# Seven half products for a second expert's first layer, and shared row buffers for attention

## Chip, cores and metric

The kernel runs on one core of a Trainium2 chip. Times are device microseconds (us) of that core, the median of several runs. The engines are TensorE (PE, with its weight loads as PEld), VectorE (DVE), ScalarE (ACT), GpSimd (POOL) and SyncE (SP), which issues most of the transfers to memory; they run beside each other and wait for each other by semaphores.

## What is computed

Attention with eight heads, three over all earlier keys and five over a window of 64 keys and four sinks, and behind it a layer of four experts, each of two matrix products with a relu between them, weighted by given probabilities.

```python
# attention: q, k, v are (4, 8, 768, 64)
scores = scale * np.matmul(q, k.transpose(0, 1, 3, 2))
scores = np.where(mask[None, :, :, :], scores, -1000000000.0)
a = softmax(scores)                       # (cut: written out in the reference)
attn_out = np.matmul(a, v)
# experts: x is (3072, 512), w1 (4, 512, 1024), w2 (4, 1024, 512)
p = domain_probs / (domain_probs.sum(-1, keepdims=True) + 1e-09)
for e in range(E):
    h = np.maximum(x @ w1[e], 0.0)
    out += p[:, e:e + 1] * (h @ w2[e])
```

## The kernel before

There are 24 tiles of 128 tokens. Attention works on eight groups of three tiles. The first four tiles go through the experts plainly; the other twenty go as ten *pairs* of tiles. The steps of attention for later groups are put between the steps of the pairs, by a plan of estimated times, so that TensorE always has work.

A pair has two layers. In layer 1 the inputs, scaled by the expert's probability, are multiplied with w1. For experts 0 to 2 this is done plainly, as four steps of eight products of 128 x 128 weights with 256 columns. For expert 3 (`EW`) it is done in Winograd's form of Strassen's scheme: the matrices are cut into 2 x 2 blocks, and seven products of half size stand in for eight. Each of the seven is eight TensorE instructions of 128 columns. The scheme needs sums of blocks of the weights (made once), of the inputs and of the results (made for every pair, on VectorE and ScalarE). Layer 2 uses the same scheme for all experts at once.

```python
EW = E - 1
t1sb = pers.tile([P, 3, KH, FN], FP16, name="t1sb")       # sums of expert 3's weights
...
def plain_layer1(e):
    xs = scaled(e)
    for f0 in range(0, FTP, 2):
        ps = bank()
        for f in range(2):
            for ct in range(DMP):
                nc.tensor.matmul(out=ps[:, f * PC : (f + 1) * PC], ...)   # 256 columns
        nc.scalar.activation(out=blocks[...], in_=ps..., func=AF.Relu)
        step_done()
        yield 2 * DMP * mm_ns(PC), 0.5
...
def winograd_layer1():
    ...
    x = pO.tile([P, DM], FP32, name="pO", bufs=2)
    y = pO.tile([P, DM], FP32, name="pO", bufs=2)
    # keep: a ScalarE copy of a bank; add: a VectorE add of bank and copy, and a maximum with 0
    product(x, w1_part(0, 0), x_part(0, 0), True)
    keep(0, x)
    yield ns, 0.5
    product(y, w1_part(1, 0), x_part(0, 1), True)
    add(0, y, 0)
    yield ns, 0.5
    product(x, t(1), x_sum(1), False)
    keep(1, x)
    yield ns, 0.5
    product(y, t(0), x_sum(0), True)
    keep(2, y)
    minus(x_part(0, 1), x_part(0, 1), x_sum(1))
    yield ns, 0.5
    product(x, w1_part(0, 1), x_part(1, 0), False)
    add(2, x, 3)
    yield ns, 0.5
    product(y, w1_part(1, 1), x_part(0, 1), False)
    add(1, y, 2)
    yield ns, 0.5
    product(x, t(2), x_part(1, 1), False)
    nc.scalar.activation(out=block(1), in_=x..., func=AF.Relu)
    yield ns, 0.5

scale_inputs(nt0, 1)
...
products = winograd_layer1()
n = 0
for e in range(E - 1):
    if e == 1:
        scale_inputs(nt0, 2)
    elif e == 2 and nxt is not None:
        load_probs(nxt)
    for step in plain_layer1(e):
        yield step
        step = next(products, None) if n > 1 else None   # one half product behind a plain step
        n += 1
        if step is not None:
            yield step
    if e:
        sums += input_sums(...)       # S1 = A21 + A22 and S3 = A11 - A21, in two pieces each
...
# layer 2: seven products of 16 instructions of 256 columns; beside them S2, S4,
# and the scaling of the next pair's inputs for experts 0 and 3
```

`product(..., False)` adds onto what is in the bank, so it must come after the reader of the bank's earlier content. Two lines record many operations: `minus` (L939) is every difference, and `scale_inputs` (L1066) every scaling.

Attention's rows of q and k come by transfers of GpSimd's queue into buffers of their own, and SyncE's transposing transfers turn them into `qT`, of which there are two, and `kT`:

```python
def load_q(b, c):
    q16[b, c] = att.tile([P, 3, H, D], FP16, name="q16", bufs=1)
    load_by_rows(q, q16[b, c], b, c)
def load_k(b, c):
    k_rows[b, c] = att.tile([P, 3, H, D], FP16, name="k_rows", bufs=1)
    load_by_rows(k, k_rows[b, c], b, c)
def alloc_qT(b, c):
    qTs[b, c] = att.tile([P, HP, CH], FP16, name="qT", bufs=2)
...
# in attention(), after the fourth of eight heads (group 2 and later):
if n == 3 and more and g > 1:
    transpose_rows(*more)             # kT, then qT, of the next group
```

Of the kernel before, what the change touches and what calls it, by code (L numbers as in the profile page):

```python
# [1 line left out]

# [15 lines left out]
def kernel(  # L18
# [33 lines left out]
    nc = tc.nc  # L52
# [58 lines left out]
    EW = E - 1  # L111
    KH, FN = DMP // 2, F // 2
    t1sb = pers.tile([P, 3, KH, FN], FP16, name="t1sb")
# [18 lines left out]
    XS = 3 * DMP * 2 * P  # L132
    early = moe.tile([P, XS], FP16, name="early", tag="xs", bufs=1)
# [19 lines left out]
    v_sinks = pers.tile([NS, 1, NSH * P], FP16, name="v_sinks")  # L153
# [62 lines left out]
    def load_q(b, c):  # L216
        q16[b, c] = att.tile([P, 3, H, D], FP16, name="q16", bufs=1)
        load_by_rows(q, q16[b, c], b, c)
# [12 lines left out]
    def load_k(b, c):  # L231
        k_rows[b, c] = att.tile([P, 3, H, D], FP16, name="k_rows", bufs=1)
        load_by_rows(k, k_rows[b, c], b, c)
# [3 lines left out]
    def alloc_qT(b, c):  # L237
        qTs[b, c] = att.tile([P, HP, CH], FP16, name="qT", bufs=2)
# [12 lines left out]
    def transpose_rows(b, c):  # L251
        alloc_qT(b, c)
        for x, xr, at in ((kT, k_rows[b, c], P), (qTs[b, c], q16[b, c], 0)):
            for j in range(3):
                nc.sync.dma_start(
                    out=x[:, :, at + j * P : at + (j + 1) * P],
                    in_=xr[:, j, :, :].rearrange("p h d -> p (h d)"),
                    transpose=True,
                )
# [226 lines left out]
    qt16 = att.tile([P, H, 3, D], FP16, name="q16", bufs=1)  # L486
# [38 lines left out]
    def attention(b, c):  # L525
# [109 lines left out]
        def scores(h):  # L635
            hp = h // 2
            es_of[h] = []
            for cols, parts, masks in score_tiles(h):
                ps = bank()
                if first and not es_of[h]:  # L640
                    warm_up(ps, {0: 5, 2: 8}.get(h, 0), P)
                ns = 0
                for n, (t, o, q0, nq) in enumerate(parts):
                    nc.tensor.matmul(  # L644
                        out=ps[:, o : o + nq],
                        lhsT=key_tile(b, c, h, t),
                        rhs=qTs[b, c][:, hp, q0 : q0 + nq],
                        start=(n == 0 or not first),
                        stop=not first,
                        skip_group_check=first,  # L650
                    )
                    ns += mm_ns(nq)
                if first:
                    for m, mo, o0, o1 in masks:
                        bias = bC if m is mC else bSf
                        nc.tensor.matmul(
                            out=ps[:, o0:o1], lhsT=ident16,
                            rhs=bias[:, mo : mo + o1 - o0],
                            start=False, stop=True, skip_group_check=True,
                        )  # L660
                es = att.tile([P, 512], FP16, name="es", bufs=8)
                nc.scalar.activation(  # L662
                    out=es[:, 0:cols], in_=ps[:, 0:cols], func=AF.Exp, scale=SC
                )
                for m, mo, o0, o1 in () if first else masks:
                    nc.vector.tensor_tensor(  # L666
                        out=es[:, o0:o1],
                        in0=es[:, o0:o1],
                        in1=m[:, mo : mo + o1 - o0],
                        op=ALU.mult,  # L670
                    )
                es_of[h].append((es, parts))
                if first:
                    tick(LAG)
                yield ns
# [158 lines left out]
        else:  # L834
# [16 lines left out]
            for n, h in enumerate(order):  # L851
# [12 lines left out]
                if n == 3 and more and g > 1:  # L864
                    transpose_rows(*more)
                if not by_dma and n in (1, 3):
                    yield from transposes({1: 3, 3: 2}[n])
            if more:
                if g == 1:
                    load_probs(pair0)  # L870
                    transpose_rows(*more)
# [75 lines left out]
    def w1_part(j, k):  # L947
        return w1sb[:, EW * DMP + j * KH : EW * DMP + (j + 1) * KH, k * FN : (k + 1) * FN]

    def first_weight_sums():  # L950

        t = [t1sb[:, n, :, :] for n in range(3)]
        return [
            lambda: minus(t[0], w1_part(0, 1), w1_part(0, 0)),
            lambda: minus(t[1], w1_part(1, 1), t[0]),
            lambda: minus(t[2], w1_part(1, 0), t[1]),
            lambda: minus(w1_part(0, 1), w1_part(1, 1), w1_part(0, 1)),
        ]
# [91 lines left out]
    def scaled(e):  # L1050
        n = 2 if e == EW else e % 2
        x = xs_of[0][:, n * DMP * PC : (n + 1) * DMP * PC]
        return x.rearrange("p (c x) -> p c x", c=DMP)

    def scale_inputs(nt0, e):

        if xs_of[0] is None:
            xs_of[0] = moe.tile([P, XS], FP16, name="xs", tag="xs", bufs=1)
# [11 lines left out]
    def x_part(i, j):  # L1070
        return scaled(EW)[:, j * KH : (j + 1) * KH, i * P : (i + 1) * P]
# [6 lines left out]
    def scaled_sums():  # L1078
        nc.vector.tensor_tensor(
            out=x_sum(0), in0=x_part(1, 0), in1=x_part(1, 1), op=ALU.add  # L1080
        )
        minus(x_sum(1), x_sum(0), x_part(0, 0))
        minus(x_part(1, 0), x_part(0, 0), x_part(1, 0))

    def input_sums(k0, k1):
        k = slice(k0, k1)

        def s1():
            nc.vector.tensor_tensor(
                out=S1[:, k, :], in0=A21[:, k, :], in1=A22[:, k, :], op=ALU.add  # L1090
            )

        return [
            s1,
            lambda: minus(S3[:, k, :], A11[:, k, :], A21[:, k, :]),
        ]
# [4 lines left out]
    def pair_steps(nt0, nxt):  # L1101

        sums = []

        def step_done():
            if sums:
                sums.pop(0)()

        def plain_layer1(e):
            xs = scaled(e)  # L1110
            for f0 in range(0, FTP, 2):
# [19 lines left out]
                step_done()  # L1131
                yield 2 * DMP * mm_ns(PC), 0.5

        def winograd_layer1():

            s = moe.tile([P, 4 * HN], FP32, name="s1", tag="sums", bufs=1)
            kept = [s[:, (n % 2) * HT * P : (n % 2 + 1) * HT * P] for n in range(3)]
            x = pO.tile([P, DM], FP32, name="pO", bufs=2)
            y = pO.tile([P, DM], FP32, name="pO", bufs=2)
# [17 lines left out]
            def block(n):  # L1157
                return blocks[:, n, EW * HT : (EW + 1) * HT, :]
# [12 lines left out]
            def t(n):  # L1171
                return t1sb[:, n, :, :]

            product(x, w1_part(0, 0), x_part(0, 0), True)
            keep(0, x)
            yield ns, 0.5
            product(y, w1_part(1, 0), x_part(0, 1), True)
            add(0, y, 0)
# [6 lines left out]
            minus(x_part(0, 1), x_part(0, 1), x_sum(1))  # L1185
            yield ns, 0.5
            product(x, w1_part(0, 1), x_part(1, 0), False)
            add(2, x, 3)
            yield ns, 0.5
            product(y, w1_part(1, 1), x_part(0, 1), False)  # L1190
            add(1, y, 2)
            yield ns, 0.5
            product(x, t(2), x_part(1, 1), False)
# [5 lines left out]
        scale_inputs(nt0, 1)  # L1199
        if nt0 == pair0:  # L1200
            sums.append(lambda: last_weight_sum(E - 1))
        products = winograd_layer1()
        n = 0
        for e in range(E - 1):
            if e == 1:
                scale_inputs(nt0, 2)
            elif e == 2 and nxt is not None:
                load_probs(nxt)
            for step in plain_layer1(e):
                yield step  # L1210
                step = next(products, None) if n > 1 else None
                n += 1
                if step is not None:
                    yield step
            if e:
                sums += input_sums(0, 2 * HT) if e == 1 else input_sums(2 * HT, 4 * HT)
        for op in sums:
            op()
# [3 lines left out]
        s = s.rearrange("p (n x) -> p n x", n=4)  # L1222
        x = pO.tile([P, DM], FP32, name="pO", bufs=2)[:, 0:HN]
        y = pO.tile([P, DM], FP32, name="pO", bufs=2)[:, 0:HN]
# [36 lines left out]

        def fourth_sum(n):
            k = slice(n * KT // 2, (n + 1) * KT // 2)
            minus(S4[:, k, :], A12[:, k, :], S2[:, k, :])
# [9 lines left out]
        add(0, y, 0, 0)  # L1274
        yield half
        yield from product(x, S2, t(1), False)
        keep(1, x)
        fourth_sum(0)
        yield half
        yield from product(y, S1, t(0), True)  # L1280
        keep(2, y)
        fourth_sum(1)
# [8 lines left out]
        if nxt is not None:  # L1291
            scale_inputs(nxt, EW)
# [6 lines left out]
        if nxt is not None:  # L1299
            scaled_sums()  # L1300
# [8 lines left out]
    def moe_steps():  # L1309
        for e in range(E):  # L1310
            if e == 1:
                turn_probs()
            yield from plain_steps(0, 3, e, lambda: xT[0], (e % 2) * FTP * CH)
            weight_sums(e)
        sums = first_weight_sums()
        for e in range(E):
            n0 = (e % 2) * FTP * P
            for n, step in enumerate(plain_steps(3, 1, e, lambda: xT[1][:, :, 0:P], n0)):
                yield step
                if n == FTP - 1:  # L1320
                    sums[e]()
            if e + 1 < E:
# [3 lines left out]
                    lambda: scale_inputs(pairs[0], EW),  # L1326
                    scaled_sums,
# [14 lines left out]
    def loads(a):  # L1342
        b, c = divmod(a, NCH)
        load_k(b, c)
        load_q(b, c)
# [6 lines left out]
    PAIR = (E - 1) * FTP * DMP * mm_ns(PC) + 28 * FTP // 4 * mm_ns(P) + 7 * KT * mm_ns(HN)  # L1352
# [91 lines left out]
```

The softmax here doesn't subtract the row's maximum and nothing guards it: scores larger than these inputs give would overflow.

## Time and profile before

| | before |
|---|---|
| time, median of 3 | 382.71 us (381.86 to 383.02) |
| span of the profiled execution | 380.0 us |
| busy: POOL | 110.8 us |
| TensorE's clock | 1.0 throughout |
| first pair begins | 91.4 us |
| VectorE idle ahead of its adds of half products (L1161), waiting for TensorE | 16.3 us |

The span is what the profiler recorded of one execution, and is a little shorter than the time. A busy share tells how much of the span an engine worked, not whether others waited for it; the chain that ended last tells that. A group of instructions is one line of the program, one engine and one form of tile: its total, its count, its mean, and how long the engine stood idle just ahead of it. The times of single stages are read from the chain and from stretches of the trace.

### The profile page before, as it was taken

How to read it: one execution, taken by the hardware profiler on the slowest of the kernel's cores; microseconds unless marked ns; L12 is line 12 of the kernel's file. 1: busy time of each engine (PE TensorE's matmuls, PEld its weight loads, DVE VectorE, ACT ScalarE, POOL GpSimd, SP SyncE). 2: the span in 40 equal slices, each digit the busy share in tenths (PEclk: the TensorE clock that was granted, in tenths of full speed). 3: DMA queues.
4: the chain of work that ended last, by engine and by line, in shares of the span. 5: the costliest groups of instructions: out<-in, count | busy, mean ns of one | idle time of the engine just before them, and what ended most of it. 6: DMA issues, size and time to landing. Idle time of an engine off the chain costs nothing.

```text
span 380.0 us, 9930 instructions
## 1 busy us (share of the span) xinstructions
PE 370.4 (97%) x4054; PEld 311.5 (82%) x4054; DVE 267.9 (70%) x590; ACT 230.3 (61%) x476; POOL 110.8 (29%) x152
## 2 busy tenths in 40 slices
PE   7989999999999999999999999999999999999996
PEld 4755556577998998899988998999988998998995
DVE  7745687598978678967667767967767757665560
ACT  4853567656776876665764775675665684541630
POOL 8932662854139029113800118203100000000000
PEclk9999999999999999999999999999999999999999
DMA  9999999999499969965950869965510210110001
GB/s 165 155 208 201 183 192 190 149 191 136 67 136 127 133 99 100 145 124 38 155 81 16 109 123 84 142 127 43 84 54 16 68 58 0 58 57 29 28 2 55
DMA packets 127193, 39.20 MB, mean 103 GB/s; under 512 B 116232, under 2 KB 120876, under 8 KB 127148
## 3 DMA queue, kind: packets, MB, share of 16 engines
q0 software_dynamic: 86816, 19.01, 56.8%
q1 hardware_dynamic: 38732, 19.18, 22.9%
q8 instruction: 31, 0.51, 0.6%
q10 hardware_dynamic: 1600, 0.39, 0.5%
q14 instruction: 14, 0.11, 0.1%
HBM read 44.88 MB, written 6.34 MB: 135 GB/s over the span
## 4 chain that ended last, share of the span: by engine, by line
PE 85%; DMA 7%; POOL 3%; DVE 3%; ACT 1%; issue 0%; POOLq 0%
PE pO L1228 32%; PE pA L1115 27%; PE pO L1145 8%; DMA w2sb<-in_moe_w_dram 7%; PE pO L1004 6%; PE pA L644 5%; PE pA L983 4%; PE pV L756 2%; PE pV L692 2%; POOL vS L302 1%; DVE xs L1066 1%; POOL vR L296 1%; ACT es L662 1%; DVE kS L282 0%; POOL early L441 0%
## 5 line engine op out<-in xcount | busy, mean ns | idle before, releaser
L1115 PE MATMUL pA<-xs,w1sb 128*128 128x256 f16 x960 | 119.1, 273 | 0.2 <-DVE xs L1066 0.2
L1228 PEld LDWEIGHTS <-hA 128*128 128x128 f16 x1120 | 106.5, 98 | 12.8
L1115 PEld LDWEIGHTS <-w1sb 128*128 128x128 f16 x960 | 89.7, 98 | 9.8 <-DVE xs L1066 0.4
L1124 ACT ACTIVATE hA<-pA 128x512 f16<-128x512 f32 x120 | 71.4, 597 | 37.9 <-PE pA L1115 36.2
L662 ACT ACTIVATE es<-pA 128x384 f16<-128x384 f32 (+2 forms) x122 | 59.0, 511 | 32.1 <-PE pA L644 28.0
L1228 PE MATMUL pO<-w2sb,hA 128*128 128x256 f16 x640 | 78.1, 273 | 0.0
L298 POOL DMA_DIRECT2D vS<-in_v_dram x30 | 29.6, 989 | 124.7 <-PE pV L756 117.3
L1228 PE MATMUL pO<-tsb,hA 128*128 128x256 f16 x480 | 58.9, 272 | 0.0
L1066 DVE TENSOR_TENSOR xs<-xT,pB 128x1024 f16<-128x1024 f16 (+1 forms) x52 | 49.4, 969 | 0.0
L939 DVE TENSOR_TENSOR hA<-hA 128x1024 f16<-128x1024 f16 x60 | 39.7, 685 | 0.8
L996 ACT ACTIVATE hA<-pA 128x384 f16<-128x384 f32 (+1 forms) x64 | 22.3, 386 | 20.3 <-PE pA L983 19.5
L1161 DVE TENSOR_TENSOR hA<-pO,s 128x512 f16<-128x512 f32 x30 | 20.6, 687 | 17.2 <-PE pO L1145 16.3
L983 PE MATMUL pA<-xT,w1sb 128*128 128x384 f16 (+1 forms) x256 | 31.7, 273 | 0.1
L1004 PE MATMUL pO<-w2sb,hA 128*128 128x512 f16 x128 | 30.5, 379 | 0.6 <-DMA w2sb<-in_moe_w_dram 0.6
L779 DVE TENSOR_TENSOR xT<-pV,rc 64x384 f16<-64x384 f32 x37 | 20.5, 554 | 14.1 <-ACT rc L784 11.8
L774 ACT ACTIVATE rc<-pV,eps 64x384 f32<-64x384 f32 x37 | 21.3, 575 | 9.1 <-PE pV L756 8.5
L983 PEld LDWEIGHTS <-w1sb 128*128 128x128 f16 x256 | 19.3, 98 | 8.4 <-issue 0.5
L1145 PE MATMUL pO<-xs,w1sb 128*128 128x128 f16 x320 | 24.4, 219 | 0.0
L644 PE MATMUL pA<-qT,kR 128*128 128x384 f16 (+2 forms) x120 | 22.9, 278 | 0.9 <-ACT qT L555 0.4
L1249 DVE TENSOR_TENSOR o<-pO,s 128x256 f32<-128x256 f32 x30 | 12.7, 422 | 14.6 <-PE pO L1228 11.8
L666 DVE TENSOR_TENSOR es<-es,mS 128x384 f16<-128x384 f16 (+1 forms) x40 | 13.4, 343 | 13.4 <-ACT es L662 13.3
L1004 PEld LDWEIGHTS <-hA 128*128 128x128 f16 x128 | 11.9, 98 | 12.6 <-issue 0.8
(131 smaller groups left out, 460.3 us busy)
## 6 DMA issues: line engine op xcount, KB each, us to landing
pB<-p_rows SPq DMA_DIRECT2D x10, 512.0 KB, 3.4
out_dram<-o SPq DMA_DIRECT2D x19, 256.0 KB, 4.6
w1sb<-in_moe_w_dram POOLq DMA_DIRECT2D x8, 512.0 KB, 10.3
w2sb<-in_moe_w_dram POOLq DMA_DIRECT2D x4, 1024.0 KB, 13.3
vS<-in_v_dram POOLq DMA_DIRECT2D x30, 112.0 KB, 3.7
k_rows<-in_k_dram POOLq DMA_DIRECT2D x18, 128.0 KB, 4.6
q<-in_q_dram POOLq DMA_DIRECT2D x18, 128.0 KB, 5.6
vR<-in_v_dram POOLq DMA_DIRECT2D x24, 48.0 KB, 5.3
```

The lines of the kernel that those rows point to most:

```text
L298: gp.dma_start(out=t[:, :, own_v(h)], in_=windows_of(v, b, h, c))
L644: nc.tensor.matmul(out=ps[:, o : o + nq], lhsT=key_tile(b, c, h, t), rhs=qTs[b, c][:, hp, q0 : q0 + nq], start=(n == 0 or not first), stop ...
L662: nc.scalar.activation(out=es[:, 0:cols], in_=ps[:, 0:cols], func=AF.Exp, scale=SC)
L939: nc.vector.tensor_tensor(out=out, in0=a, in1=b, op=ALU.subtract)
L983: nc.tensor.matmul(out=pss[ft][:, 0:cols_n], lhsT=w1sb[:, e * DMP + ct, ft * P : (ft + 1) * P], rhs=x[:, ct, :], start=(n == 0), stop=(n = ...
L996: nc.scalar.activation(out=hs[:, ft, :], in_=ps[:, 0:cols_n], func=AF.Relu)
L1004: nc.tensor.matmul(out=ps_o, lhsT=hs[:, ft, j * P : (j + 1) * P], rhs=w2sb[:, e * FTP + ft, :], start=(ft == 0), stop=(ft == FTP - 1),)
L1066: nc.vector.tensor_tensor(out=o, in0=xin, in1=pb.to_broadcast([P, DMP, n, P]), op=ALU.mult)
L1115: nc.tensor.matmul(out=ps[:, f * PC : (f + 1) * PC], lhsT=w1sb[:, e * DMP + ct, (f0 + f) * P : (f0 + f + 1) * P], rhs=xs[:, ct, :], start= ...
L1124: nc.scalar.activation(out=blocks[:, b0 : b0 + 2, k0 : k0 + 2, :].rearrange("p t f x -> p f t x"), in_=ps.rearrange("p (f t x) -> p f t x" ...
L1145: nc.tensor.matmul(out=ps[:, f * P : (f + 1) * P], lhsT=w[:, ct, f * P : (f + 1) * P], rhs=a[:, ct, :], start=(first and f == 0 and ct == ...
L1228: nc.tensor.matmul(out=ps, lhsT=a[:, k, :], rhs=b(k), start=(first and k == 0), stop=(k == KT - 1), skip_group_check=not first,)
```

## The change

Expert 2's first layer is to be done in the seven half products too, so that two experts are plain and two are not. Expert 2's weight sums are made once, beside the plain tiles. The 14 half products of a pair stand two by two (sometimes one) ahead of each of the eight plain steps, first those of expert 3, then those of expert 2, which uses the two banks exchanged; the second product of each expert goes into one of the four banks of `bank()`. S1 is made in four pieces, one for each expert, and S3 moves to layer 2 as S3 = A22 - S2. All four experts' scaled inputs now have space of their own.

To make room for the added sums and inputs, attention's rows of q and k share one buffer (`rows`), `qT` has one buffer in place of two, `es` (the exponentials) has seven in place of eight, and the sinks of v lie in a part of another tile. So k is transposed after the fourth head as before, q is loaded behind that, and is transposed after the last head's scores.

```diff
-    EW = E - 1
+    EW = (E - 1, E - 2)
-    t1sb = pers.tile([P, 3, KH, FN], FP16, name="t1sb")
+    t1sb = pers.tile([P, len(EW), 3, KH, FN], FP16, name="t1sb")
...
     def load_q(b, c):
-        q16[b, c] = att.tile([P, 3, H, D], FP16, name="q16", bufs=1)
+        if b * NCH + c == NCH:
+            q16[b, c] = moe.tile([P, 3, H, D], FP16, name="q16", tag="o", bufs=1)
+        else:
+            q16[b, c] = att.tile([P, 3, H, D], FP16, name="rows", bufs=1)
...
-        k_rows[b, c] = att.tile([P, 3, H, D], FP16, name="k_rows", bufs=1)
+        k_rows[b, c] = att.tile([P, 3, H, D], FP16, name="rows", bufs=1)
...
-        qTs[b, c] = att.tile([P, HP, CH], FP16, name="qT", bufs=2)
+        qTs[b, c] = att.tile([P, HP, CH], FP16, name="qT", bufs=1)
...
-                es = att.tile([P, 512], FP16, name="es", bufs=8)
+                es = att.tile([P, 512], FP16, name="es", bufs=7)
...
                 if n == 3 and more and g > 1:
-                    transpose_rows(*more)
+                    transpose_k(*more)
+
+                    load_q(*more)
...
             if more:
                 if g == 1:
                     load_probs(pair0)
-                    transpose_rows(*more)
+                    transpose_k(*more)
+                transpose_q(*more)
             for h in waiting:
                 yield from values(h)
...
-            product(y, w1_part(1, 0), x_part(0, 1), True)
-            add(0, y, 0)
+            z = bank()
+            product(z, w1_part(e, 1, 0), x_part(e, 0, 1), True)
+            add(0, z, 0)
...
+        a, b = (winograd_layer1(e, *y) for e, y in zip(EW, (banks, banks[::-1])))
+        n01 = itertools.chain(plain_layer1(0), plain_layer1(1))
+        for steps, op in (
+            ((a, a, n01), lambda: scale_inputs(nt0, EW[1])),
+            ((a, a, n01), lambda: scale_inputs(nt0, 1)),
+            ((a, n01), lambda: scaled_sums(EW[1])),
+            ((a, a, n01), lambda: load_probs(nxt) if nxt is not None else None),
+            ((b, b, n01), lambda: first_sum(0)),
+            ((b, b, n01), lambda: first_sum(EW[0])),
+            ((b, n01), lambda: last_weight_sum(E - 1) if nt0 == pair0 else None),
+            ((b, b, n01), None),
+        ):
+            for x in steps:
+                yield next(x)
+            if op is not None:
+                op()
+        first_sum(1)
+        first_sum(EW[1])
...
+        y = pO.tile([P, DM], FP32, name="pO", bufs=2)[:, 0:HN]
         x = pO.tile([P, DM], FP32, name="pO", bufs=2)[:, 0:HN]
-        y = pO.tile([P, DM], FP32, name="pO", bufs=2)[:, 0:HN]
...
+        def third_sum(n):
+            k = slice(n * KT // 2, (n + 1) * KT // 2)
+            minus(S3[:, k, :], A22[:, k, :], S2[:, k, :])
...
-        fourth_sum(0)
+        third_sum(1)
...
-    PAIR = (E - 1) * FTP * DMP * mm_ns(PC) + 28 * FTP // 4 * mm_ns(P) + 7 * KT * mm_ns(HN)
+    PAIR = 2 * FTP * DMP * mm_ns(PC) + 2 * 7 * HT * KH * mm_ns(P) + 7 * KT * mm_ns(HN)
```

`PAIR` is the plan's estimate of a pair's length; the plan's other numbers stay.

## The prediction, as it stood before the result

> **What bounds the kernel now.** I read the page's shares first, then the groups with shapes kept apart, then the chain that ended last, then busy time by stage, then the order of instructions in one pair. The shares and the chain's summary:
>
> ```profile
> PE 370.4 (97%) x4054; PEld 311.5 (82%) x4054; DVE 267.9 (70%) x590; ACT 230.3 (61%) x476; POOL 110.8 (29%) x152
> ...
> PE 85%; DMA 7%; POOL 3%; DVE 3%; ACT 1%; issue 0%; POOLq 0%
> ```
>
> TensorE (PE) is busy 97% of the span and carries 85% of the chain, so only less TensorE work, or a wait put into TensorE's order, moves the time. VectorE (DVE) is second with 70%. The groups that carry the first layer of the pairs and the vector work beside it:
>
> ```profile
> L1115 PE MATMUL pA<-xs,w1sb 128*128 128x256 f16 x960 | 119.1, 273 | 0.2 <-DVE xs L1066 0.2
> ...
> L1145 PE MATMUL pO<-xs,w1sb 128*128 128x128 f16 x320 | 24.4, 219 | 0.0
> ...
> L1161 DVE TENSOR_TENSOR hA<-pO,s 128x512 f16<-128x512 f32 x30 | 20.6, 687 | 17.2 <-PE pO L1145 16.3 <-ACT s L1155 0.6
> ...
> L1167 DVE TENSOR_SCALAR hA<-hA 128x512 f16<-128x512 f16 x30 | 9.8, 328 | 1.0
> ```
>
> The means (273, 219 ns) contain the pipeline and are no cost. The cost comes from the chain in the last pair, where no attention lies between:
>
> ```profile
> 350.93 2.62 PE pA L1115 x24
> ...
> 364.54 12.24 PE pO L1228 x112
> ```
>
> 24 plain products of 256 columns take 2.62 us: 0.873 us for a step of eight, 109.2 ns each. Layer 1 lasts 364.54 - 350.93 = 13.61 us and holds 12 plain steps and 7 half products, so a half product (eight products of 128 columns) takes (13.61 - 12 x 0.873) / 7 = 0.447 us, 55.9 ns each. All of it is TensorE without a gap. Busy time by stage (columns: stretch, its length, then PE, PEld, DVE, ACT) for layer 1 of the first and the last pair:
>
> ```profile
> 91.44:106.42 14.98, 14.98 (x202) 13.85 (x200) 13.62 (x35) 11.68 (x22) 1.03 (x1) 1.00 0.57 80
> ...
> 350.93:364.54 13.61, 13.61 (x154) 12.52 (x153) 7.38 (x14) 8.86 (x16) 0.00 (x0) 1.00 0.08 28
> ```
>
> VectorE is busy 7.4 us of 13.6 in a pair alone, but already 13.6 of 15.0 in the first pair, where a group of attention runs beside it. TensorE waits for it in neither.
>
> [...] The trace agrees (55.9 and 109.2), so a product of half the width costs 51%, and 7 half-size products cost less than the 8 they replace. [...] In the stretches of the trace that I read, vector instructions ran in program order, one at a time. [...] the trace has 0.685 for 1024 and 0.285 for 256, whose straight line gives 0.42 too.
>
> **The change part by part.** *TensorE, per pair:* removed are 4 plain steps, 4 x 0.873 = 3.49 us; added are 7 half products, 7 x 0.447 = 3.13 us. Saved: 0.36 us a pair, 3.6 us for ten pairs. Nothing else of TensorE changes, so 379.1 us if nothing new waits. That is 0.95% and the ceiling of the gain.
>
> *ScalarE, per pair:* minus 4 x 0.597, plus 3 copies x 0.583 and one relu of 0.593: even.
>
> *VectorE, per pair:* plus 3 adds x 0.687, 3 maxima x 0.328, one difference x 0.283, three scaled sums (0.286 + 0.292 + 0.283): 4.2 us; cutting the first sum into four pieces of 0.42 in place of two of 0.685 adds 0.3. The third sum moves from layer 1 to layer 2. So 4.5 us x 10, and 4 x 0.68 for the weight sums of expert 2: 267.9 + 48 = about 316 us. On average it fits (82% of the span); but pairs 0 to 7 held 176 us of VectorE in 233.7 us (by stage), and would hold 212 in 231: 92%.
>
> *The new order in a pair alone.* Between the end of the second half product and the first product of expert 2, which overwrites the bank of the sixth, TensorE has 4 plain steps and 5 half products: 4 x 0.873 + 5 x 0.447 = 5.73 us. In that time VectorE must run, in this order and by start-to-start times of the last pair: 0.27 from TensorE's end to the add, add and maximum 0.94, scaling for expert 2 1.14, difference 0.21, scaling for expert 1 1.14, add and maximum 0.94, three scaled sums 0.74, and the add that frees the bank 0.69. Sum 6.07. TensorE waits 6.07 - 5.73, with the release some 0.36 us. In the second half expert 2's products have only 3.7 us of VectorE work beside 6.6 of TensorE and don't wait. So in a pair alone the wait eats the gain.
>
> *With attention.* Layer 1 of pairs 0 to 7 held 86.6 us of VectorE, 27.5 more than eight times 7.38; TensorE's stretches are 118.8 long, 9.9 more than eight times 13.61. If half of each falls in the first half of the layer, VectorE's chain there grows by 13.8 and TensorE by 5.0: up to 8.8 us of further waiting. I take half, 4.4, since part of that work can run ahead while the chain still waits for TensorE.
>
> *Buffers.* q can be loaded only after k's transposes have read the shared rows, and transposed only after the last scores, as qT has one buffer. In group 3 the k transposes are issued to 102.7:
>
> ```profile
> 98.07 4.64 SPq L255 DMA_TRANSPOSE kT<-k_rows  x3
> 102.80 3.84 SPq L255 DMA_TRANSPOSE qT<-q  x3
> ```
>
> Landing takes 4.0 from issue, so the last lands at about 105.5; three q loads to 108.1, landing (5.6 from issue) at about 112.9; three transposes, the last issued at 115.3, landed at 119.3. Group 3's first scores ran at 116.08: up to 3 us of waiting. For group 4 the same sum gives 148.5 against 148.03; groups 5 and 7 have 20 us of slack, group 6 some 2. I take 1.5 in all, as these issues may land faster (2.4 is the least seen) and TensorE will itself be later.
>
> Sum of everything: 382.7 - 3.6 + 3.6 + 4.4 + 1.5 = 388.6.
>
> **Rivals.** *A: all hidden.* VectorE starts its work early enough and only TensorE's saving shows: 379.1. For it: the shares (VectorE far from full), and the change's own care (a spare bank for the second product, banks exchanged for the second expert, the third sum moved to layer 2). Against it: 6.07 over 5.73, which holds in every pair. *B: VectorE becomes the bound beside attention*, in full: 8.8 and 3.0 in place of 4.4 and 1.5, 394.5. For it: 13.62 of 14.98 us busy in the first pair before anything is added. Against it: layer 2 has loose waits and can take the overhang. *C: ScalarE's copies come late.* A copy now has one half product and one plain step, 1.32 us, before its bank is accumulated onto, where it had 2.19; an exponential of 0.5 and a relu of 0.6 ahead of it would make it late by 0.3, at perhaps five places: 1 or 2 us. *D: the transposes of q come last everywhere* (the next group held for each): plus 3 to 6 us.
>
> **Range and chances.** I weigh A (379.1) at 0.4 against my sum (388.6) at 0.6: 384.8, rounded to 384.6. A range of 8 in 10: 379.5 to 391. Faster by over 2% (below 375.1) would need more than the TensorE saving: 0.02. Slower by over 2% (above 390.4) needs B or D nearly whole: 0.19. Within 2%: 0.79.
>
> **What would show it.** Plain products fall from 960 to 640 and half products rise from 560 to 1120; PE instructions 4054 to 4294; VectorE about 714 instructions, 312 to 318 us. Layer 1 of the last pair stays near 13.6 us, with a TensorE gap of 0.3 to 0.4 ahead of expert 2's first half product, ended by a vector add; if there is no gap and it lasts 13.25, A is right. In the first pair the gap is above 1 us. TensorE's first scores of group 3 would be held by qT. I am wrong if TensorE's idle time in the pairs stays near nothing, or if the waits lie at ScalarE's copies.

## The result and the profile after

The changed kernel takes 398.72 us (median of 6 runs, 398.02 to 400.37) against 382.74 for the kernel before (median of 6): a ratio of 1.0424, 95% interval 1.0401 to 1.0447. It is slower by 4.2%, and outside the predicted range of 379.5 to 391.

The page of the changed kernel: busy shares, the chain's shares, and the groups of layer 1. Lines have moved: half products are L1144 (L1145 before), their adds L1160, the scaling of inputs L1078, all differences L951.

```profile
PE 372.4 (94%) x4294; PEld 312.3 (79%) x4294; DVE 306.9 (77%) x714; ACT 229.6 (58%) x476; POOL 110.4 (28%) x152
...
PE 56%; DVE 26%; DMA 9%; issue 3%; ACT 3%; POOL 1%; SPq 1%; DVEq 0%; ACTq 0%; POOLq 0%
...
L1115 PE MATMUL pA<-xs,w1sb 128*128 128x256 f16 x640 | 82.9, 273 | 0.0
...
L1144 PE MATMUL pO<-xs,w1sb 128*128 128x128 f16 x480 | 36.6, 219 | 2.4 <-DVE hA L1160 1.8
...
L1160 DVE TENSOR_TENSOR hA<-pO,s 128x512 f16<-128x512 f32 x40 | 27.4, 686 | 6.6 <-PE pO L1144 6.0
```

Counts are as worked out: 640 plain products, 4294 TensorE and 714 VectorE instructions. VectorE's time, 306.9 us, is below the 312 to 318 that were forecast: the forecast added durations, as if VectorE's instructions ran one at a time, and neighbours overlap a little (below, a scaling of 1.22 us begins at 98.86 and the next instruction at 100.00, 0.08 before its end). VectorE is busy only 77%, and yet it carries 26% of the chain where it had 3%. The longest of TensorE's waits (us in total, times, longest), and the group of the seventh half products, from the groups with shapes kept apart:

```profile
PE pO L1144 <- DVE hA L1160: 9.7, 15, 1.5
```

```profile
L1144 PE MATMUL pO<-xs,t1sb 128*128 128x128 f16 x160 | 12.2, 219 | 8.2 <-DVE hA L1160 7.9
```

Of 9.7 us that TensorE waits for adds, 7.9 stand ahead of the product that uses the scaled inputs and the summed weights, the seventh: it accumulates onto the bank that the second add, that of the fifth product, must have read. Busy time by stage, layer 1 of the first and of the last pair:

```profile
92.75:110.04 17.29, 14.93 (x224) 13.74 (x220) 15.62 (x44) 11.60 (x22) 3.67 (x4) 1.00 0.89 112
...
366.96:380.69 13.73, 13.55 (x178) 12.54 (x176) 10.54 (x24) 8.85 (x16) 0.00 (x0) 1.00 0.09 33
```

The first pair's layer 1 grew from 14.98 to 17.29 us, the last pair's from 13.61 to 13.73. What happens in the first pair is seen in the order of time (start, duration, engine, line, tile; in brackets the idle time just before and who ended it):

```profile
98.73 0.62 PE L1144 MATMUL pO<-xs,w1sb 128*128 128x128 f16 x8 [0.50 <-DVE xs L951]
...
98.86 1.22 DVE L1078 TENSOR_TENSOR xs<-xT,pB 128x1024 f16<-128x1024 f16 x1
100.00 0.68 DVE L1160 TENSOR_TENSOR hA<-pO,s 128x512 f16<-128x512 f32 x1
...
100.73 0.61 PE L1144 MATMUL pO<-xs,t1sb 128*128 128x128 f16 x8 [1.20 <-DVE hA L1160]
...
102.32 0.68 DVE L1160 TENSOR_TENSOR hA<-pO,s 128x512 f16<-128x512 f32 x1
...
103.06 0.61 PE L1144 MATMUL pO<-xs,w1sb 128*128 128x128 f16 x8 [0.66 <-DVE hA L1160]
```

The product at 98.73 is the sixth; it waited for a difference of inputs. The seventh waits until the add that began at 100.00 is through, and that add stood behind a scaling of 1.22 us for expert 1. The first product of expert 2, at 103.06, waits for the next add, the third.

VectorE is late from the start of the layer. In the first pair it has attention's work ahead of the first add, the copies of keys above all; in the last pair it only waits for ScalarE's copy:

```profile
93.39 0.61 DVE L291 COPY kS<-kT 64x1736 f16<-64x1736 f16 x1
...
96.20 0.68 DVE L1160 TENSOR_TENSOR hA<-pA,s 128x512 f16<-128x512 f32 x1
...
368.27 0.69 DVE L1160 TENSOR_TENSOR hA<-pA,s 128x512 f16<-128x512 f32 x1 [0.50 <-ACT s L1154]
```

So the first add begins 3.45 us into the layer, against 1.31 in the last pair. From there to the third add VectorE has no idle time of even 0.08 us, in any of the ten pairs: in this half of the layer it is the bound engine.

The whole loss by place, from the first product of each layer to that of the next (attention's steps between them are counted in; all in us):

| | start of the first pair | ten layers 1 | ten layers 2 and the end | span |
|---|---|---|---|---|
| before | 91.28 | 143.95 | 144.77 | 380.0 |
| after | 92.75 | 157.39 | 146.16 | 396.3 |
| difference | +1.5 | +13.4 | +1.4 | +16.3 |

TensorE's saving, 3.6, lies in layer 1, so the waits there are 17.1. The idle time that the trace records in these layers is less, 12.9, since it counts from the modelled end of a product (219 ns after its start, where the next could start after 56). Attention's share of the layers hardly moved: 235 of its TensorE instructions lie in them, against 232 before.

### The profile page after: what moved, and what is told of

It reads as the page before. It is cut to its first block, busy times and chain, and to the rows that moved or that the text cites. A ratio compares the mean times of both kernels' runs of the same rounds, so it can differ in the third digit from the quotient of the medians.

```text
span 396.3 us, 10589 instructions
## 1 busy us (share of the span) xinstructions
PE 372.4 (94%) x4294; PEld 312.3 (79%) x4294; DVE 306.9 (77%) x714; ACT 229.6 (58%) x476; POOL 110.4 (28%) x152
## 4 chain that ended last, share of the span: by engine, by line
PE 56%; DVE 26%; DMA 9%; issue 3%; ACT 3%; POOL 1%; SPq 1%; DVEq 0%; ACTq 0%; POOLq 0%
PE pO L1228 24%; PE pA L1115 10%; PE pO L1144 8%; DVE xs L1078 7%; DMA w2sb<-in_moe_w_dram 7%; DVE hA L1160 4%; PE pA L653 4%; PE pO L1017 3%; PE pA L996 3%; DMA qT<-rows 2%; DVE kS L291 2%; DVE es L675 1%; PE pV L765 1%; PE pV L701 1%; ACT es L671 1%
## 5 line engine op out<-in xcount | busy, mean ns | idle before, releaser
L1228 PEld LDWEIGHTS <-hA 128*128 128x128 f16 x1120 | 106.2, 98 | 12.6
L1115 PE MATMUL pA<-xs,w1sb 128*128 128x256 f16 x640 | 82.9, 273 | 0.0
L1124 ACT ACTIVATE hA<-pA 128x512 f16<-128x512 f32 x80 | 47.8, 599 | 29.5 <-PE pA L1115 27.3
L1115 PEld LDWEIGHTS <-w1sb 128*128 128x128 f16 x640 | 58.9, 98 | 5.5
L1078 DVE TENSOR_TENSOR xs<-xT,pB 128x1024 f16<-128x1024 f16 (+1 forms) x52 | 49.5, 970 | 0.0
L1144 PEld LDWEIGHTS <-w1sb 128*128 128x128 f16 x640 | 39.6, 98 | 5.9 <-issue 3.4
L1144 PEld LDWEIGHTS <-t1sb 128*128 128x128 f16 x480 | 29.3, 98 | 13.1 <-issue 10.2
L951 DVE TENSOR_TENSOR hA<-hA 128x1024 f16<-128x1024 f16 x60 | 39.0, 684 | 0.2
L1144 PE MATMUL pO<-xs,w1sb 128*128 128x128 f16 x480 | 36.6, 219 | 2.4 <-DVE hA L1160 1.8
L212 POOL DMA_DIRECT2D rows<-in_q_dram x15 | 13.4, 900 | 86.8 <-DMA kT<-rows 86.8
L1154 ACT COPY s<-pO 128x512 f32<-128x512 f32 x60 | 33.6, 591 | 6.1 <-PE pO L1144 3.7
L1160 DVE TENSOR_TENSOR hA<-pO,s 128x512 f16<-128x512 f32 x40 | 27.4, 686 | 6.6 <-PE pO L1144 6.0
L996 PEld LDWEIGHTS <-w1sb 128*128 128x128 f16 x256 | 19.2, 98 | 8.2 <-issue 0.5
```

The lines of the kernel that those rows point to most:

```text
L951: nc.vector.tensor_tensor(out=out, in0=a, in1=b, op=ALU.subtract)
L996: nc.tensor.matmul(out=pss[ft][:, 0:cols_n], lhsT=w1sb[:, e * DMP + ct, ft * P : (ft + 1) * P], rhs=x[:, ct, :], start=(n == 0), stop=(n = ...
L1078: nc.vector.tensor_tensor(out=o, in0=xin, in1=pb.to_broadcast([P, DMP, n, P]), op=ALU.mult)
L1115: nc.tensor.matmul(out=ps[:, f * PC : (f + 1) * PC], lhsT=w1sb[:, e * DMP + ct, (f0 + f) * P : (f0 + f + 1) * P], rhs=xs[:, ct, :], start= ...
L1124: nc.scalar.activation(out=blocks[:, b0 : b0 + 2, k0 : k0 + 2, :].rearrange("p t f x -> p f t x"), in_=ps.rearrange("p (f t x) -> p f t x" ...
L1144: nc.tensor.matmul(out=ps[:, f * P : (f + 1) * P], lhsT=w[:, ct, f * P : (f + 1) * P], rhs=a[:, ct, :], start=(first and f == 0 and ct == ...
```

## Experiments

The theories are: **Q**, the order of VectorE's queue and the short distances between a half product and the next use of its bank; **B**, the shared buffers; **C**, ScalarE's copies come late; **L**, VectorE's load as a whole; **D**, formed after the second set, distances and added VectorE work together. The *distance* of a bank is the TensorE work between a half product and the next product that uses its bank. All kernels were measured beside the kernel before on the same chip, whose medians were 381.8 to 382.5; the changed kernel's 398.72 stood beside 382.74, so differences from it are good to about 0.9 us. Stage sums of one execution each, cut as above:

| kernel | time | ratio to before (95%) | start | layers 1 | layers 2 |
|---|---|---|---|---|---|
| before, rows shared | 385.88 | 1.0081 (1.0056 to 1.0106) | 91.26 | 143.73 | 148.21 |
| after, no scaling for expert 1 | 390.51 | 1.0195 (1.0160 to 1.0229) | 92.86 | 149.46 | 146.58 |
| after, that scaling a pair earlier | 393.95 | 1.0289 (1.0251 to 1.0328) | 92.82 | 148.83 | 150.85 |
| after, attention out of layer 1 | 410.03 | 1.0715 (1.0660 to 1.0771) | 91.69 | 150.05 | 165.96 |
| before, more VectorE work | 383.74 | 1.0046 (1.0029 to 1.0063) | 90.75 | 145.95 | 144.80 |
| after, VectorE's order changed | 400.04 | 1.0461 (1.0438 to 1.0484) | 92.50 | 158.24 | 147.66 |
| after, scaling earlier, q's own rows | 399.62 | 1.0451 (1.0429 to 1.0473) | 93.24 | 150.76 | 153.90 |
| after, maxima on ScalarE | 417.06 | 1.0932 (1.0890 to 1.0973) | 91.85 | 175.09 | 147.16 |
| before, halves two by two | 384.65 | 1.0074 (1.0046 to 1.0102) | 93.56 | 146.01 | 144.83 |
| before, two by two and more work | 392.26 | 1.0267 (1.0228 to 1.0307) | 91.39 | 154.24 | 144.77 |
| after, one copy less | 398.84 | 1.0431 (1.0395 to 1.0466) | 92.73 | 157.76 | 146.91 |
| after, both places mended | 392.66 | 1.0292 (1.0258 to 1.0325) | 92.16 | 148.27 | 150.07 |

### The buffers alone

The kernel before with attention's buffer part of the change and nothing else.

```diff
-        k_rows[b, c] = att.tile([P, 3, H, D], FP16, name="k_rows", bufs=1)
+        k_rows[b, c] = att.tile([P, 3, H, D], FP16, name="rows", bufs=1)
-        qTs[b, c] = att.tile([P, HP, CH], FP16, name="qT", bufs=2)
+        qTs[b, c] = att.tile([P, HP, CH], FP16, name="qT", bufs=1)
...  # load_q, load order, transposes and es as in the change
```

> The kernel before with the buffer part alone: q and k rows share one buffer, qT has one, es has seven; layer 1 stays as before. If the queue of VectorE in layer 1 makes most of the loss (theory Q), this costs only what layer 2 of the second pair lost by late transposes of q, 2 to 4 us over the kernel before: 384.5 to 387. If late rows and transposes make most of it (theory B), 393 to 399.

Measured 385.88 us, 3.4 over its neighbours. TensorE's waits in order of time:

```profile
117.41 0.38 PE L652 MATMUL pA<-qT,kR 128*128 128x128 f16 x2 [1.19 <-DMA qT<-rows]
151.47 0.38 PE L652 MATMUL pA<-qT,kR 128*128 128x128 f16 x2 [2.06 <-DMA qT<-rows]
```

Both are first scores of a group that wait for q's transposes, in layer 2 of the first and the second pair (+1.35 and +2.10 us); all other stages stay. So B is real, and not the main loss. It is about as large as TensorE's whole saving, though. In the changed kernel TensorE comes later there: it waits for q's transposes only once, 0.77 us in layer 2 of the second pair.

### Expert 1's scaling left out

This kernel leaves out the scaling of expert 1's inputs after the first pair.

```diff
-            ((a, a, n01), lambda: scale_inputs(nt0, 1)),
+            ((a, a, n01), lambda: scale_inputs(nt0, 1) if nt0 == pair0 else None),
```

> The changed kernel without the scaling of expert 1's inputs after the first pair (they keep the first pair's), which takes 1.14 us out of VectorE's queue ahead of the add that the seventh half product waits for. Theory Q (the order in VectorE's queue): the waits at the seventh product go, 6 to 10 us off the changed kernel's 398.7: 389 to 393. Theory B (buffers) or theory C (ScalarE's copies): at most 1 us off.

390.51 us, 8.2 less, for the scalings of nine pairs, 9.9 us of VectorE. In the last pair TensorE no longer waits at all in layer 1:

```profile
360.01:373.27 13.26, 13.26 (x177) 12.51 (x176) 9.48 (x23) 8.77 (x16) 0.00 (x0) 1.00 0.09 33
```

13.26 us against the 13.25 that the counts give (13.61 - 0.36): the saving on TensorE is real where nothing waits. In pairs beside attention 9 us of waiting remain in layer 1 (149.46 against 143.95 - 3.64 = 140.3), so this scaling is not all of it.

### The same work a pair earlier

```diff
         fourth_sum(0)
         fourth_sum(1)
+        if nxt is not None:
+            scale_inputs(nxt, 1)
```

(and the scaling taken from layer 1 but for the first pair.)

> The changed kernel with that scaling moved into layer 2 of the pair before: the same VectorE work in all, another place. Theory Q in its narrow form (it is the place in the queue): nearly as good as leaving it out, 390 to 394. Theory L (VectorE's load in the pairs as a whole, wherever it lies): 396 to 399. Theories B and C: 398.

393.95 us, in the range given for Q. Layer 1 gains as much as by leaving the work out (148.83), but layer 2 grows by 4.7 (150.85 against 146.16): about half of the gain is given back. In layer 2 this is mostly VectorE's work arriving late for attention (copies of keys, 1.5 of the 2.4 us below; the other 0.9 lie ahead of the pairs) and for the next pair's inputs:

```profile
PE pA L653 <- DVE kR L275: 2.4, 2, 1.5
PE pO L1144 <- DVE xs L1078: 2.0, 3, 1.0
```

Neither Q in its narrow form nor L is right alone: the place matters, and neither of the two places that were run is free.

### Attention kept out of layer 1

```diff
-                yield 2 * DMP * mm_ns(PC), 0.5
+                yield 2 * DMP * mm_ns(PC), 0.1
-    PSHARE = 1.57
+    PSHARE = 2.0
```

(and 0.1 for the half products too.)

> The changed kernel with attention's steps nearly kept out of layer 1 (weight 0.1 in place of 0.5 there, 2.0 in place of 1.57 in layer 2). Theory Q: layer 1 waits some 0.5 us in each pair, layer 2 grows by the attention moved and waits little: 389 to 395. Theory L: the waits move into layer 2, 397 to 402.

410.03 us, worse than either theory said. Of attention's 235 TensorE instructions in the ten layers 1, 32 are left. Layer 1 gains only 7.3, mostly these products, and keeps its waits (12.2 us recorded, of 12.9): VectorE still comes to the layer with attention's work queued ahead, and in four pairs the first add begins 2.0 to 3.5 us into it with no idle time of VectorE ahead of it, as in the first pair:

```profile
95.14 0.68 DVE L1160 TENSOR_TENSOR hA<-pA,s 128x512 f16<-128x512 f32 x1
```

That layer began at 91.69. Layer 2 loses 19.8, the moved products among it. The shared rows show there: with attention packed closer, q's transposes are waited for in three groups, by 7.9 us.

```profile
PE pA L653 <- DMA qT<-rows: 7.9, 3, 4.0
```

### VectorE's load without the distances

The kernel before, with idle vector work.

```diff
         def step_done():
             if sums:
                 sums.pop(0)()
+            nc.vector.tensor_tensor(
+                out=spare, in0=w1sb[:, 0, 0:512], in1=w1sb[:, 0, 512:1024], op=ALU.add
+            )
```

> The kernel before with one more vector sum of 512 elements (0.42 us, on a spare tile, nothing waits for it) behind each of the twelve plain steps of a pair: 5.0 us of VectorE a pair, somewhat more than the change adds, and no new dependence. Theory Q (the change's short distances between a half product and the next use of its bank): 383 to 386, since before a bank's reader has 2.19 us. Theory L (VectorE's load beside attention is enough): 390 to 400.

383.74 us. The group shows that the work is there, and the page's shares that VectorE is now busier (309 us) than in the changed kernel (307):

```profile
L1110 DVE TENSOR_TENSOR vS<-w1sb 128x512 f16<-128x512 f16 x120 | 50.4, 420 | 1.6
```

A sum of 512 elements took 0.420 us, as the prediction's straight line from 0.285 us at 256 and 0.685 at 1024 has it. 50 us more of VectorE cost 1.4. Theory L falls: the load alone, spread over a layer with distances of 2.19 us, is hidden.

### VectorE's order changed

```diff
-            ((a, a, n01), lambda: scale_inputs(nt0, 1)),
-            ((a, n01), lambda: scaled_sums(EW[1])),
-            ((a, a, n01), lambda: load_probs(nxt) if nxt is not None else None),
+            ((a, a, n01), lambda: scaled_sums(EW[1])),
+            ((a, n01), None),
+            ((a, a, n01), lambda: (scale_inputs(nt0, 1), load_probs(nxt) ...)),
```

> The changed kernel with two of VectorE's jobs exchanged in its queue and nothing else: the three scaled sums come ahead of the add that the seventh half product waits for, the scaling for expert 1 behind expert 3's last add. Theory Q: the wait at the seventh product shrinks from about 1.2 to 0.7 us and the first plain step of expert 1 waits some 0.3 instead: 394 to 397. Theory L: 398 to 400.

400.04 us, no gain. The waits for adds are halved, and the same time is lost at expert 1's first plain step:

```profile
PE pA L1115 <- DVE xs L1078: 6.2, 6, 1.6
PE pO L1144 <- DVE hA L1160: 4.8, 7, 1.0
```

In the first half of the layer VectorE is the slower engine (it had no idle time there in the changed kernel); the order only picks which product waits.

### q's rows in a buffer of their own

The kernel with the scaling a pair earlier, q's rows separate and loaded early; to make room es has six buffers and rc one.

```diff
-            q16[b, c] = att.tile([P, 3, H, D], FP16, name="rows", bufs=1)
+        q16[b, c] = att.tile([P, 3, H, D], FP16, name="q16", bufs=1)
-                es = att.tile([P, 512], FP16, name="es", bufs=7)
+                es = att.tile([P, 512], FP16, name="es", bufs=6)
...
```

> The kernel with expert 1's scaling in the pair before (393.95), with q's rows in a buffer of their own again, loaded early (es six, rc one buffer to make room; qT stays one). If the shared rows cost what they cost in the kernel before (3.4 us), 390 to 392; if those waits are only traded for waits on VectorE, 393 to 395.

399.62 us, worse by 5.7 and outside both ranges. The wait for q's transposes is gone, but the next one behind it, for the copies of keys, takes its place (5.4 us in 3 waits against 2.4 in 2). The smaller es and rc were changed with it, so what made those copies late stays open.

### The maxima on ScalarE

```diff
-                nc.vector.tensor_scalar(
-                    out=block(b), in0=block(b), scalar1=0.0, scalar2=None, op0=ALU.max
-                )
+                nc.scalar.activation(out=block(b), in_=block(b), func=AF.Relu)
```

> The changed kernel with the maximum behind each add of a half product done by ScalarE: 2.0 us less VectorE and some 3.5 us more ScalarE a pair. Theory L: 390 to 394. Theory C (ScalarE's copies come late): 400 to 406, as its queue is longer. Theory Q narrow (only what stands ahead of the add in the queue counts): one maximum of 0.2 to 0.3 us less ahead of it, 395 to 397.

417.06 us, by far more than any theory said.

```profile
L1166 ACT ACTIVATE hA<-hA 128x512 f16<-128x512 f16 x60 | 37.7, 629 | 49.5 <-DVE hA L1160 48.9
```

ScalarE, which takes 0.629 us for it where VectorE took 0.314 in the changed kernel, now stands idle 49 us in its queue until VectorE's adds are through, and its copies behind come late: TensorE waits 14.6 us for them. With the two engines' queues joined, the kernel takes 18.3 us more, although VectorE is busy 18 us less (288.7 against 306.9).

### The distances without the load, and both

The kernel before with its seven half products standing two by two, at the changed kernel's distances; VectorE's work as before.

```diff
-                step = next(products, None) if n > 1 else None
+                for _ in range((0, 0, 2, 2, 1, 2)[n] if n < 6 else 0):
+                    yield next(products)
                 n += 1
-                if step is not None:
-                    yield step
...
-            product(y, w1_part(1, 0), x_part(0, 1), True)
-            add(0, y, 0)
+            z = bank()
+            product(z, w1_part(1, 0), x_part(0, 1), True)
+            add(0, z, 0)
```

> The kernel before, one expert in half products as it was, but these stand two by two with the changed kernel's distances (the second product into a bank of its own): from the fifth product's end to the seventh TensorE has 1.32 us in place of 2.19. VectorE's work is that of before. If short distances alone make the waits: 386 to 392. If it takes distances and added VectorE work together (theory D): 382 to 385.

The second kernel adds the idle sums to it.

> The same with the twelve idle vector sums of 0.42 us in each pair. Theory D (distances and VectorE's work together): clearly more than the sum of the two alone (1.4 us for the sums), 387 to 394. If only the named waits of the second expert matter: 383 to 386.

384.65 and 392.26 us, both in theory D's ranges. Over the kernel before: the load alone 0.46%, the distances alone 0.74%, both 2.67% (2.28 to 3.07). By layer 1: 2.0, 2.1 and 10.3 us. The two together cost over twice their sum, with no second expert and no shared buffer. In the second kernel most waits stand where the changed kernel has them, ahead of the seventh product:

```profile
102.96 0.61 PE L1150 MATMUL pO<-xs,t1sb 128*128 128x128 f16 x8 [1.72 <-DVE hA L1166]
166.33 1.01 PE L1150 MATMUL pO<-xs,t1sb 128*128 128x128 f16 x8 [2.18 <-DVE hA L1166]
```

Around the end of the second TensorE's mean clock was 0.50 for 3.40 us (see the last section), and the slower products there make some 1.5 of the 10.3 (an estimate from the products' starts); 8.8 is still over twice the sum of 4.1. The one execution of this kernel with a mean clock of 1.000 took 390.47.

This is theory D, shown: load and distance together, without anything else of the change, make TensorE wait in layer 1 where each alone hardly does. The idle sums put 5.0 us of VectorE into each layer 1, though, and the change only 3.2 (10.54 against 7.38 us in the last pair), so the changed kernel's 17.1 aren't taken apart by this. What the second expert's own chain and the scalings bunched in the first half add wasn't separated.

### One copy of ScalarE less

This kernel leaves out the copy of the third half product; the add takes the fourth's copy instead.

```diff
             product(x, t(1), x_sum(1), False)
-            keep(1, x)
...
-            add(1, y, 2)
+            add(2, y, 2)
```

> The changed kernel without the copy of the third half product (the add that needs it takes the fourth's copy): two copies, 1.2 us, less on ScalarE in each pair, and the fifth product waits for no copy. Theory C (ScalarE's copies are what TensorE and VectorE wait for): 392 to 395. Theory D: ScalarE stands only here and there in the chain, 396 to 398.5.

398.84 us with 8 us less on ScalarE, and layer 1 at 157.76: nothing changed, slightly above what D said. So this copy, which stands ahead of the fifth product, costs nothing. The first copy does cost something, and was not tested. In the changed kernel's fourth and eighth pair it ends 0.9 us late, and VectorE's first add with it:

```profile
191.85 0.69 DVE L1160 TENSOR_TENSOR hA<-pA,s 128x512 f16<-128x512 f32 x1 [0.91 <-ACT s L1154]
```

TensorE's third and fourth products wait for ScalarE too, by the group's recorded idle time:

```profile
L1144 PE MATMUL pO<-kS,t1sb 128*128 128x128 f16 x320 | 21.3, 219 | 2.4 <-DVE kS L951 1.0 <-ACT es L671 0.8 <-ACT s L1154 0.6
```

Theory C falls as the main cause; a few us of the 17.1 may be its.

### The two places mended

Scaling for expert 1 a pair earlier, for the first pair too, and expert 2's weight sums one expert earlier.

```diff
-            sums = first_weight_sums(EW[1])[:3] if e == E - 1 else []
+            sums = first_weight_sums(EW[1])[:3] if e == EW[1] else []
...
+                    if e == E - 1:
+                        scale_inputs(pairs[0], 1)
```

> The changed kernel with expert 1's scaling in the pair before for every pair, the first too, and expert 2's weight sums made one expert earlier. The wait ahead of the seventh product in the first pair (2 us) and half of the 1.4 us lost before the pairs go: 391 to 393, against 393.95 without these two. The shared rows' 3.4 us stay, so it doesn't reach the kernel before (382.5).

392.66 us, against 393.95 with the scaling moved alone: the first pair's layer 1 is 0.8 shorter and the pairs begin 0.7 earlier, which is no more than starts differ from one execution to another (next section). Of the versions that do all the work it is the fastest that was run, and does not reach the kernel before.

## Why the prediction was wrong

**TensorE's saving** (0.36 us a pair): right. It is seen in full, 13.26 us for the last pair's layer 1, once the wait is taken away; so is the ceiling of 0.95%.

**The wait in a pair alone** (6.07 against 5.73 us, 0.36 a pair): right in size, incomplete in place. The last pair's layer 1 took 13.73, so 0.48 over 13.25. By the products' starts 0.34 of it stands ahead of expert 2's first product, as forecast, and 0.15 ahead of the seventh, which the sum passed over: it counted only the chain up to the bank of the sixth.

**The waits beside attention**: this is the term that failed, "up to 8.8 us of further waiting. I take half, 4.4". Measured are 17.1 us of waits in layer 1, and ten times 0.5 of them are the pair alone; so some 12 stand where 4.4 was taken, above even the 8.8 called the most. (Cut at the first product of each layer, as in the table above, layer 1 of pairs 0 to 7 was 116.7 us long and held 85.6 of VectorE, not 118.8 and 86.6; the same working then gives 9.4.) Halving rested on "part of that work can run ahead while the chain still waits for TensorE". The trace shows the reverse. Against the last pair, the first add begins late by 10.1 us in all ten pairs together: 8.0 in four pairs in which VectorE has attention's work queued ahead of it, and most of the rest behind ScalarE's late copy. From the first add to the third, attention's work makes only 5.2 more. So two thirds of the lateness is there before the chain that the sum counted begins. The kernel with attention out of layer 1 agrees: the first add is still late, by 8.5 us in all, and the wait at the seventh product stays. The mechanism, the queue of VectorE ahead of a bank's next use, was the predicted one; that it takes load and short distances together is measured by the kernels in which they cost 1.4 and 2.8 us alone and 10.4 together.

**The start**: missed. Expert 2's weight sums, 2.7 us, were only added to VectorE's total. Their stage had VectorE busy 15.6 of 19.3 us already; two sums now stand in a row ahead of the copies of keys that a group's first scores wait for, where one stood, and TensorE waits 0.83 us there. The pairs begin 1.5 us later, of which 0.4 is there by 85 us. The size is not clear of chance: where the code ahead of the pairs is the kernel before's, they begin at 90.75, 91.28, 91.39 and 93.56.

```profile
86.35 0.69 DVE L951 TENSOR_TENSOR t1sb<-w1sb,t1sb 128x1024 f16<-128x1024 f16 x1
86.95 0.69 DVE L951 TENSOR_TENSOR w1sb<-w1sb 128x1024 f16<-128x1024 f16 x1
87.56 0.51 DVE L275 COPY kR<-kT 64x768 f16<-64x768 f16 x2
```

**The buffers** (1.5 us): alone they cost 3.4, at the two groups that were named. The sum came near (up to 3 and 0.5 were worked out), but by luck, since the waits recorded are 1.19 and 2.06. In the changed kernel 0.77 is left, at group 4 and not at group 3, as TensorE comes later anyway: the reason given for taking less was right, and 1.5 was still too much.

**The weighing**: rival A, all hidden, was given 0.4. It had against it a sum that held in every pair, and no run supports it. Without that weight the text's own sum was 388.6, still 10 short. Rival B, named at 394.5 and given little, was nearest, and VectorE as the bound engine beside attention is what the trace shows. Rival C is not the main loss; its 1 or 2 us may be there, at the first copy, and are untested. Rival D comes true only when attention is packed closer.

**VectorE's layer 2** "has loose waits and can take the overhang": wrong. Of the 8.6 us that layer 1 gained by moving one scaling there, layer 2 gave back 4.7.

**The terms together**: -3.6 saved, 4.8 in a pair alone, some 12 beside attention, 1.5 at the start and 1.4 in layer 2 make the 16.3 us of the span. The text's own sum had -3.6, 3.6, 4.4, nothing and 1.5.

## What to carry to other kernels

VectorE, busy 70% before and 77% after, was no reserve, since its results were waited for at short distance: 1.32 us of TensorE's work in place of 2.19 ahead of the seventh product. Ask for each result how much work of the bound engine lies between its source and its next use, and what else can stand ahead of it in the queue, also from the stage before. Added work (1.4 us) and shortened distances (2.8) were each nearly free here and cost 10.4 together, so the two have to be judged at once. And when a saving is 3.6 us, the buffers it needs must be priced alone first: here they cost 3.4 by themselves.

## What was not expected of the hardware

TensorE's granted clock, 1.00 through all pairs in the profiles of before and after, fell when attention was kept out of layer 1. The stage of that kernel in which TensorE waited 3.96 us for q's transposes had a mean of 0.86 (the number ahead of the last two):

```profile
142.83:167.35 24.52, 19.68 (x226) 16.17 (x224) 16.30 (x42) 13.37 (x27) 10.59 (x12) 0.86 1.27 88
```

Eight products of 256 columns took 1.04 us ahead of that wait and 1.92 behind it:

```profile
144.35 1.04 PE L1228 MATMUL pO<-w2sb,hA 128*128 128x256 f16 x8
...
161.23 1.92 PE L1228 MATMUL pO<-w2sb,hA 128*128 128x256 f16 x8
```

So that wait cost more than its own 3.96 us. The clock fell at shorter waits too. In the kernel with halves two by two and more work its mean was 0.50 over the 3.40 us from 165.95, in which the wait of 2.18 ended, while behind the wait of 2.06 in the kernel with shared rows it stayed at 1.00:

```profile
165.95:169.35 3.40, 3.02 (x24) 2.45 (x24) 2.18 (x6) 0.87 (x2) 0.00 (x0) 0.50 0.59 102
```

```profile
151.50:154.90 3.40, 3.40 (x32) 2.97 (x32) 1.68 (x5) 1.58 (x3) 2.92 (x4) 1.00 0.60 38
```

And in the kernel with the maxima on ScalarE eight products of 256 columns took 1.90 us behind two waits of 1.07 and 0.86 us. The page of that kernel gives TensorE's clock, in tenths, an 8 in this fortieth of the span and a 9 in all others.

```profile
96.03 1.03 PE L1115 MATMUL pA<-xs,w1sb 128*128 128x256 f16 x8 [1.07 <-DVE hA L1160]
97.92 0.62 PE L1144 MATMUL pO<-xs,w1sb 128*128 128x128 f16 x8 [0.86 <-ACT s L1154]
...
98.68 1.90 PE L1115 MATMUL pA<-xs,w1sb 128*128 128x256 f16 x8
```

So in these runs the length of one wait does not tell whether the clock falls: it stayed behind 2.06 us and fell behind 1.07 and 0.86. What decides it was not looked into.
